# Score visits of six PSUM banks across head pairs, in a fused attention and low-rank mixer kernel

## The chip, the cores and the metric

The kernel runs on one NeuronCore of a Trainium2 chip. Five engines take part, each with its own instruction stream: TensorE (PE, with its weight loads as PEld) multiplies matrices into the eight banks of PSUM, VectorE (DVE) and ScalarE (ACT) empty those banks, GpSimd (POOL) issues the input loads, and SyncE (SP) issues the transposing DMAs and the stores. Engines wait for each other through semaphores. The metric is the device time of one execution in microseconds; smaller is better.

## The reference

Eight batches, eight heads, 576 tokens of 64 elements, and 16 beacon keys and values that stand ahead of the tokens. First attention with a causal mask on the tokens, then a low-rank mix over the token axis, then a two-layer MLP, with two residual sums:

```python
k_all = concatenate([beacon_k, k], axis=2); v_all = concatenate([beacon_v, v], axis=2)
a = softmax(where(causal, -1e9, q @ k_all.T / sqrt(64)))
x = (a @ v_all)  # heads side by side: 8 x 576 x 512
u = x + (x.T @ U @ V).T            # U: 576 x 32, V: 32 x 576
out = u + relu(u @ w_ch1) @ w_ch2  # 512 -> 2048 -> 512
```

## The kernel before

Work goes by head pairs. A pair is two heads of a batch, four pairs to a batch, 32 in all; one pass of the loop at L896 is a slot, and slot p ends with the attention output of pair p done. Batches are numbered from 0.

**Scores.** For a pair, the transposed scores (keys down the partitions, queries along the columns) fall into four groups of 496, 464, 496 and 208 columns for each of the two heads (`groups`, L82). The third group packs pieces of three key chunks. `score_units` (L317) makes a visit of two groups: four PSUM banks (two groups by two heads), then the matmuls (L345), which use 64 rows of the array for each head, then four exponentials on ScalarE (L351), each of which empties one bank into `expt`. So a pair has two visits: groups 0 and 1, then groups 2 and 3. After both, `masks` (L321 and L323) sets what lies above the diagonal on VectorE. Four `expt` buffers hold two pairs.

**V products.** `av_unit` (L370) multiplies a head's `expt` with its values into one bank `po` (15 matmuls, L374); VectorE takes the reciprocal of the sums (L382) and writes the scaled result into `xb` (L383).

**Mixing.** When a batch is complete, `mix_units` (L395) gives four steps. `turn` has SyncE transpose `xb` into `uT` by five DMAs (L402). `head`, the first mixing products, multiplies `xb` with U into bank `qtp`, in four column strips of the array (L411). `most`, the second mixing products, multiplies that with V into four banks `ups` (L436), and VectorE adds them to `uT` in place (L423), so that this addition needs the transposes. `end` does the last 80 tokens (L449).

**MLP.** The rows of all batches form nine blocks of 512. A block is 32 units: 16 `g_unit` (four matmuls of 512 columns into `gps`, L511, then a ReLU on ScalarE, L524, or VectorE, L526) and 16 quarter units `c_unit` (four matmuls into `cps`, L537; after the fourth, an addition on VectorE, L550, and a store by SyncE, L556). The first `g_unit` of a block also transposes the block's `uT` back for that addition (`ut`, four DMAs, L505).

**Order.** All five engines keep the order in which the program writes the instructions. MLP units wait in a list `queue`; `fill(n)` takes n entries out of it and writes them. A slot writes its visits, V products and masks in turn, with nine queue entries spread between. `mix` (L746) puts the first and second mixing products into that list, the first behind 10 entries, the second behind two more, and adds empty entries. `feed` appends the blocks whose rows are complete. `pst` (L105) hands out the eight PSUM banks: a new tile takes the bank that was put on the list of emptied ones longest ago.

**Loads.** For batches 4 and up, `load_whole` (L615) loads keys and queries two batches ahead, and `turns` (L627) transposes them by ten DMAs on SyncE (L635), five in the last slot of a batch and five in the first slot of the next. `load_batch` (L607) loads the values (L217) once the V products of the batch before last have been read. The SyncE stream holds, in one order, the stores, `ut`, these ten transposes and `turn`.

Of the kernel before, what the change touches and what calls it, by code (L numbers as in the profile page):

```python
# [11 lines left out]
F32 = mybir.dt.float32  # L12
I32 = mybir.dt.int32
AF = mybir.ActivationFunctionType
# [4 lines left out]
P = 128  # L19
# [11 lines left out]
def kernel(  # L31
# [13 lines left out]
    nc = tc.nc  # L45
    B, H, S, D = q.shape
# [6 lines left out]
    NH2 = H // 2  # L53
    E = D + 1
    SK = S + Nb
    scale = float(1.0 / (D ** 0.5))
# [13 lines left out]
    SLOT = 496  # L70
# [5 lines left out]
    for c in (1, 2, 3):  # L76
# [5 lines left out]
    groups = [  # L82
        [(0, 0, q0[4], 0)],
        [(1, q0[1], S - q0[1], 0)],
        [(2, q0[2], S - q0[2], 0), (0, q0[4], nq[4], S - q0[2]), (4, q0[4], nq[4], S - q0[2] + nq[4])],
        [(3, q0[3], S - q0[3], 0)],
    ]
    gw = [max(o + w for _, _, w, o in g) for g in groups]
# [16 lines left out]
    def pst(shape, dtype, name):  # L105

        b = emptied.pop(0)
        t = psum.tile(shape, dtype, tag=f"bank{b}", name=name)
        bank_of[id(t)] = (b, t)
        return t  # L110

    def emptying(t):
        emptied.append(bank_of.pop(id(t))[0])
# [43 lines left out]
    NE = 4  # L157
    expts = [const.tile([P, EW], F16, name=f"expt{i}", tag=f"expt{i}") for i in range(NE)]
    kTs = [const.tile([P, NH2, NC * P], F16, name=f"kT{i}", tag=f"kT{i}") for i in range(2)]
# [157 lines left out]
    def score_units(c, qT, kT, ex, early=False):  # L317

        def mask_head(i):
            e4 = ex[i][:, 0:EW].rearrange("p (g w) -> p g w", w=SLOT)[:, :, 0:P]  # L320
            nc.vector.tensor_tensor(out=e4, in0=e4, in1=bigmask, op=ALU.min)  # L321
            o, n = blk[(4, 4)], nq[4]
            nc.vector.tensor_tensor(  # L323
                out=ex[i][0:n, ds(o, n)], in0=ex[i][0:n, ds(o, n)], in1=mask[0:n, 0:n], op=ALU.min
            )

        def visit(gs, idle=0, by_head=True, between=None):
            turn = [(g, i) for i in range(2) for g in gs] if by_head else [(g, i) for g in gs for i in range(2)]
            ps = {(g, i): pst([P, 512], F32, name=f"sps{i}") for g, i in turn}
            keep_warm(ps[gs[0], 0], idle)  # L330
            if early:
                for g in gs:
                    for i in range(2):
                        for ch, qa, w, o in groups[g]:
                            if ch in (g, 4):
                                n = nq[ch]
                                nc.tensor.matmul(  # L337
                                    ps[g, i][:, ds(o, n)], identb, negmask[:, min(ch, 1), 0:n],
                                    start=ch == g, stop=False, skip_group_check=True,
                                )  # L340
            for g in gs:
                for ch, qa, w, o in groups[g]:
                    for i in range(2):
                        hp = slice(D * i, D * i + D)
                        nc.tensor.matmul(  # L345
                            ps[g, i][:, ds(o, w)], kT[hp, c, ds(P * ch, P)], qT[hp, c, ds(qa, w)],
                            start=not early, stop=True, skip_group_check=early,
                        )

            def exps(g, i):  # L350
                nc.scalar.activation(  # L351
                    out=ex[i][:, ds(SLOT * g, gw[g])], in_=ps[g, i][:, 0 : gw[g]], func=AF.Exp, scale=scale
                )

            for n, (g, i) in enumerate(turn):
                if between and n == len(gs):
                    between()
                exps(g, i)
                emptying(ps[g, i])

        def masks():
            for i in () if early else range(2):
                mask_head(i)

        return [
            lambda idle=0, between=None: visit([0, 1], idle, between=between),
            lambda gs=[2, 3], by_head=True: visit(gs, 0, by_head), masks,
        ]

    def av_unit(b, h, ex, vs, xb):  # L370
        po = pst([P, NT, E], F32, name="po")
        for j in range(NT):
            for c in range(j + 1):
                nc.tensor.matmul(  # L374
                    po[:, j, :],
                    ex[0 : nk[c], ds(blk[(c, j)], P)],
                    vs[0 : nk[c], ds(c * H * E + h * E, E)],
                    start=(c == 0),
                    stop=(c == j),
                )  # L380
        r = rec[:, b * H + h, :, :]
        nc.vector.reciprocal(out=r, in_=po[:, :, D : D + 1])  # L382
        nc.vector.tensor_tensor(  # L383
            out=xb[:, :, ds(h * D, D)], in0=po[:, :, 0:D], in1=r.broadcast_to([P, NT, D]), op=ALU.mult
        )
        emptying(po)
# [216 lines left out]
    NP = B * NH2  # L603
    NBLK = B * S // 512
    Ls, qTs, xbs = {}, {}, {}
# [77 lines left out]
    def qkT_of(p):  # L683
# [8 lines left out]
            turns[0] = beacons_apart(turns[0], Ls[0][0][0], 0)  # L692
        return qkT_units(turns, qTs[b], kTs[b % 2], c, copies)

    def scores_of(p):
        b, c = divmod(p, NH2)
        return score_units(c, qTs[b], kTs[b % 2], [expts[(2 * p + i) % NE] for i in range(2)], p < NM)

    def av_of(p):
        b, c = divmod(p, NH2)  # L700
        if c == 0:
            xbs[b] = xbp.tile([P, NT, DM], F16, name="xb", tag="xb")
        return [
            lambda i=i: av_unit(b, 2 * c + i, expts[(2 * p + i) % NE], vss[b % 2], xbs[b]) for i in range(2)
        ]


    NF = 2
    NM = 5
    AHEAD = 16  # L710

    DT0 = 4
    LAG = 10
    HINT = 5

    FIRST = [3, 3, 2, 1]
# [4 lines left out]
    queue = []  # L721
    state = {"t": 0}

    def fill_turns(tr, n):
        for u in tr[:n]:
            u()
        del tr[:n]

    def fill(n):
        while n > 0 and queue:  # L730
            u = queue.pop(0)
            if u is not None:
                u()
            n -= 1

    def feed(b):

        while state["t"] < NBLK and 512 * (state["t"] + 1) <= S * (b + 1):
            t = state["t"]
            units, state["part"] = mlp_units(  # L740
                512 * t, 512, lambda i, m, t=t: rows[ds(512 * t + P * i, m), :], t % 2, t > 0, t == NBLK - 1
            )
            queue.extend(units)
            state["t"] += 1

    def mix(b):  # L746

        turned = b >= NF
        turn, head, parts = mix_units(xbs[b], S * b, turned)
        if turned:  # L750
            turn()
        n = 0 if not turned else LAG + 3 if b == B - 1 else min(LAG, len(queue) - 8)
        k = 2 if turned else 1
        most, end = parts
        rest = queue[n + k + 3 :]
        queue[:] = queue[0:n] + [head] + queue[n : n + k] + [most] + queue[n + k : n + k + 3] + [end]
        for _ in range(4):
            queue.extend(rest[:1] + [None])
            del rest[:1]
        queue.extend(rest)  # L760
        feed(b)

    with tc.manual_schedule(engines={ENG.PE, ENG.Activation, ENG.DVE, ENG.SP, ENG.Pool}):
# [11 lines left out]
        t0, sc = qkT_of(0), scores_of(0)  # L775
# [9 lines left out]
        sc = scores_of(1)  # L785
# [20 lines left out]
        for p in range(2):  # L806
# [4 lines left out]
            av = av_of(p)  # L811
            av[0]()
            sc = scores_of(p + 2)
# [79 lines left out]
            fill(1)  # L893
        regroup_of(NP1 + 2)
        tr = []
        for p in range(NP1, NP):  # L896
            b, c = divmod(p, NH2)
            if c == 0 and b + 1 < B:
                load_batch(b + 1)
            if c == (2 if b + 2 == DT0 else 1) and DT0 <= b + 2 < B:  # L900
                load_whole(b + 2)
            if c == 0 and b + 1 == DT0:
                tr = turns(b + 1)
            if c == NH2 - 1 and DT0 < b + 2 < B:
                tr = turns(b + 2)
            sc = scores_of(p + 1) if p + 1 < NP else []
            qk = qkT_of(p + 2) if p + 2 < min(NP, DT0 * NH2) else []
            av = av_of(p)
            if c == NH2 - 1 or c == 0 and b + 1 == DT0:
                fill_turns(tr, NT)  # L910
            if c == 0 and b > NF:
                mix(b - 1)
            if c == (1 if b + 1 == DT0 else 0):
                fill_turns(tr, NT)
            seq = sc[0:1] + av[0:1] + qk[0:1] + sc[1:3] + qk[1:2] + av[1:2]
            if p + 3 < min(NP, DT0 * NH2):
                seq.append(lambda p=p: regroup_of(p + 3))
            quota = QUOTA.get(b, 9)
            done = 0
            for i, u in enumerate(seq):  # L920
                u()
                want = quota * (i + 1) // len(seq)
                fill(want - done)
                done = want
# [109 lines left out]
```

## Time and profile before

| what | value |
|---|---|
| median of 3 runs | 355.72 us (355.67 to 355.79) |
| the profiled execution | 355.51 us, its span 353.9 us |
| TensorE busy | 347.2 us, 3110 matmuls |
| VectorE, ScalarE, GpSimd busy | 187.8, 166.2, 97.6 us |
| score matmuls (L345) | 34.3 us, 384 matmuls |
| exponentials (L351) | 111.1 us, 256 |
| slots 16 to 31 | about 130 to 262 us from the span's start |

The span runs from the first to the last instruction; the execution's own time is 1.6 us longer. Busy times are of one execution. The chain that ended last is followed back from the last instruction: at each step to what released it, or to the instruction before it on its engine. "Landing" is the time from a DMA's issue to its completion. An idle time in square brackets stands ahead of an instruction and names what ended it.

### The profile page before, as it was taken

The numbers are of one execution on the slowest core, as the hardware profiler recorded it, in microseconds if no ns is written. First come the engines' busy times: TensorE is split into PE (matmuls) and PEld (weight loads), VectorE is DVE, ScalarE is ACT, GpSimd is POOL, SyncE is SP. The second block draws the span as 40 slices with busy tenths as digits, with TensorE's granted clock in tenths as the row PEclk, the third lists the DMA queues.
The fourth block names the chain that finished last, engine by engine and source line by source line (L and its number), as shares of the span: only waits on it lengthen the run. The fifth ranks groups of instructions, "written<-read, shape, count | busy, mean of one in ns | idle before, by whom it ended". The sixth has DMA issues, their size and how long they took to land.

```text
span 353.9 us, 7832 instructions
## 1 busy us (share of the span) xinstructions
PE 347.2 (98%) x3110; PEld 173.5 (49%) x3110; DVE 187.8 (53%) x484; ACT 166.2 (47%) x359; POOL 97.6 (28%) x137
## 2 busy tenths in 40 slices
PE   8999999999999999999999999999999999999995
PEld 3665555455554444544444444444554444444443
DVE  4756964678967643754464457444736522313311
ACT  5967851487733663457535654466403203301400
POOL 8966803527447047305810500000000000000000
PEclk9999999999999999999999999999999999999999
DMA  9999999999999979997999992172014213013012
GB/s 181 93 195 174 157 197 172 225 143 154 111 165 148 177 101 128 163 180 89 147 139 200 130 141 65 59 109 52 31 61 102 57 59 109 12 59 101 21 58 69
DMA packets 146636, 41.89 MB, mean 118 GB/s; under 512 B 131488, under 2 KB 142080, under 8 KB 146592
## 3 DMA queue, kind: packets, MB, share of 16 engines
q0 software_dynamic: 87440, 18.18, 67.2%
q1 hardware_dynamic: 58928, 22.84, 35.5%
q8 instruction: 26, 0.43, 0.5%
q10 hardware_dynamic: 224, 0.30, 0.3%
q14 instruction: 18, 0.15, 0.2%
HBM read 37.37 MB, written 9.44 MB: 132 GB/s over the span
## 4 chain that ended last, share of the span: by engine, by line
PE 94%; DMA 2%; DVE 2%; issue 1%; ACT 1%; POOL 0%; POOLq 0%; DVEq 0%
PE gps L511 36%; PE cps L537 35%; PE po L374 9%; PE sps L345 8%; DMA st<-in_k_dram 2%; PE tps L274 1%; PE tps L280 1%; PE cph L563 1%; PE qtp L411 1%; PE sps L337 1%; PE ups L436 1%; PE ups L390 0%; DVE kT L307 0%; DVE qT L307 0%; ACT expt L351 0%
## 5 line engine op out<-in xcount | busy, mean ns | idle before, releaser
L351 ACT ACTIVATE expt<-sps 128x496 f16<-128x496 f32 (+2 forms) x256 | 111.1, 542 | 59.7 <-PE sps L345 59.7
L511 PE MATMUL gps<-uT,w 128*128 128x512 f16 x576 | 135.7, 379 | 0.1
L537 PE MATMUL cps<-w,gT 128*128 128x512 f16 x560 | 132.5, 379 | 0.0
L524 ACT ACTIVATE gT<-gps 128x512 f16<-128x512 f32 x86 | 51.9, 608 | 92.4 <-PE gps L511 90.6
L511 PEld LDWEIGHTS <-w 128*128 128x128 f16 x576 | 51.8, 98 | 59.4 <-issue 3.8
L537 PEld LDWEIGHTS <-gT 128*128 128x128 f16 x560 | 49.9, 98 | 59.3 <-issue 7.0
L526 DVE TENSOR_SCALAR gT<-gps 128x512 f16<-128x512 f32 x58 | 40.0, 690 | 47.4 <-PE gps L511 46.3
L550 DVE TENSOR_TENSOR ob<-cps,ut 128x512 f32<-128x512 f32 x31 | 21.4, 690 | 47.4 <-PE cps L537 44.4
L217 POOL DMA_DIRECT2D vs<-in_v_dram x50 | 39.5, 806 | 18.3 <-PE gps L511 4.8
L374 PEld LDWEIGHTS <-expt 128*128 128x128 f16 (+1 forms) x960 | 36.1, 98 | 14.6 <-issue 2.2
L374 PE MATMUL po<-vs,expt 128*128 128x65 f16 (+1 forms) x960 | 39.4, 194 | 0.3 <-DVE expt L321 0.3
L345 PE MATMUL sps<-qT,kT 64*128 64x80 f16 (+4 forms) x384 | 34.3, 282 | 0.6 <-DVE qT L307 0.3
L383 DVE TENSOR_TENSOR xb<-po,rec 128x320 f16<-128x320 f32 x64 | 31.5, 492 | 2.2
L321 DVE TENSOR_TENSOR expt<-expt,bigmask 128x512 f16<-128x512 f16 x54 | 22.6, 419 | 11.0 <-ACT expt L351 11.0
L382 DVE RECIPROCAL rec<-po 128x5 f32<-128x5 f32 x64 | 12.0, 188 | 25.7 <-PE po L374 25.5
L345 PEld LDWEIGHTS <-kT 64*128 64x128 f16 x384 | 11.9, 94 | 22.4 <-issue 14.4
L199 POOL DMA_DIRECT2D vs<-in_beacon_v_dram x8 | 4.3, 534 | 61.2 <-PE po L374 61.2
L623 POOL DMA_DIRECT2D st<-in_q_dram x20 | 16.9, 871 | 3.5 <-DMA vs<-in_v_dram 3.3
L423 DVE TENSOR_TENSOR uT<-ups,uT 128x496 f16<-128x496 f32 x24 | 14.5, 667 | 6.0 <-PE ups L436 3.6
L623 POOL DMA_DIRECT2D st<-in_k_dram x20 | 16.9, 879 | 0.2 <-DMA vs<-in_v_dram 0.2
L307 DVE COPY qT<-tps 128x576 f16<-128x576 f16 (+1 forms) x16 | 11.8, 735 | 3.3 <-PE tps L280 1.9
L307 DVE COPY kT<-tps 128x576 f16<-128x576 f16 (+1 forms) x16 | 11.7, 734 | 2.7 <-PE tps L280 1.9
(92 smaller groups left out, 142.6 us busy)
## 6 DMA issues: line engine op xcount, KB each, us to landing
out_dram<-ob SPq DMA_DIRECT2D x35, 256.0 KB, 2.3
vs<-in_v_dram POOLq DMA_DIRECT2D x18, 128.0 KB, 7.4
w<-in_moe_w_ch_dram POOLq DMA_DIRECT2D x4, 512.0 KB, 6.3
w<-in_moe_w_ch_dram POOLq DMA_DIRECT2D x2, 1024.0 KB, 13.9
st<-in_k_dram POOLq DMA_DIRECT2D x12, 128.0 KB, 7.2
st<-in_q_dram POOLq DMA_DIRECT2D x12, 128.0 KB, 9.8
st<-in_k_dram POOLq DMA_DIRECT2D x2, 576.0 KB, 13.0
st<-in_q_dram POOLq DMA_DIRECT2D x2, 576.0 KB, 16.2
```

Source lines behind the costliest of these rows:

```text
L217: nc.gpsimd.dma_start(out=dst[a : a + nq[j], j, :, :], in_=src[hs, ds(q0[j], nq[j]), :].rearrange("h p d -> p h d"))
L307: copy(out=whole[:, :, ds(w * a, w)], in_=ps[:, 0 : TP * w].rearrange("x (j p) -> x p j", j=w),)
L321: nc.vector.tensor_tensor(out=e4, in0=e4, in1=bigmask, op=ALU.min)
L345: nc.tensor.matmul(ps[g, i][:, ds(o, w)], kT[hp, c, ds(P * ch, P)], qT[hp, c, ds(qa, w)], start=not early, stop=True, skip_group_check=early,)
L351: nc.scalar.activation(out=ex[i][:, ds(SLOT * g, gw[g])], in_=ps[g, i][:, 0 : gw[g]], func=AF.Exp, scale=scale)
L374: nc.tensor.matmul(po[:, j, :], ex[0 : nk[c], ds(blk[(c, j)], P)], vs[0 : nk[c], ds(c * H * E + h * E, E)], start=(c == 0), stop=(c == j),)
L383: nc.vector.tensor_tensor(out=xb[:, :, ds(h * D, D)], in0=po[:, :, 0:D], in1=r.broadcast_to([P, NT, D]), op=ALU.mult)
L511: nc.tensor.matmul(g[:, 0:n], w1[:, cc, ts(dc, P)], uT[:, cc, ds(t0, n)], start=(cc == 0), stop=(cc == NCC - 1))
L524: nc.scalar.activation(out=gT["t"][:, dc, 0:n], in_=g[:, 0:n], func=AF.Relu)
L526: nc.vector.tensor_scalar_max(out=gT["t"][:, dc, 0:n], in0=g[:, 0:n], scalar1=0.0)
L537: nc.tensor.matmul(ps[:m, :], gT["t"][:, dc, ds(P * i, m)], w2[:, dc, :], start=(dc == 0), stop=turned and dc == NDC - 1, skip_group_check ...
L623: nc.gpsimd.dma_start(out=dst[a : m[j], j, :, :], in_=src[:, ds(q0[j], nq[j]), :].rearrange("h p d -> p h d"))
```

## The change

From slot 16 (batch 4) on, slots are written by `long_slot`, in a cycle of three slots with four visits:

- A visit fills six banks: three groups by two heads, and the groups of a visit may belong to two pairs. Scores of pairs 17 to 31 take 20 visits; they took 30. Each exponential still empties one bank. Visits of pair p + 2 begin in slot p.
- The mixings of batches 3 to 6 no longer go through `mix`. `mix_between` issues `turn` and holds the other steps: the first mixing products follow directly behind the next visit, the second come at a fixed place of a slot once at least 8 (`SINCE`) units have been written since `turn`, the last 80 tokens three queue entries later. The mixing of batch 7 is as before.
- V products have one MLP unit between the two heads, and one between the second and the next visit; masks come at fixed places.
- Slots write 6, 6 and 13 units in turn, where each had nine entries, some of which were mixing steps or empty.

Everything up to slot 15 is as before. The diff, cut to its core:

```diff
+    def visit(parts):
+        at = {p: (p % NH2, qTs[p // NH2], kTs[p // NH2 % 2], expts_of(p)) for p, _ in parts}
+        ps = {(p, g, i): pst([P, 512], F32, name=f"sps{i}") for p, g in parts for i in range(2)}
+        for p, g in parts:
+            c, qT, kT, _ = at[p]
+            for ch, qa, w, o in groups[g]:
+                for i in range(2):
+                    hp = slice(D * i, D * i + D)
+                    nc.tensor.matmul(
+                        ps[p, g, i][:, ds(o, w)], kT[hp, c, ds(P * ch, P)], qT[hp, c, ds(qa, w)],
+                        start=True, stop=True,
+                    )
+        for p, g in parts:
+            for i in range(2):
+                nc.scalar.activation(
+                    out=at[p][3][i][:, ds(SLOT * g, gw[g])], in_=ps[p, g, i][:, 0 : gw[g]], func=AF.Exp, scale=scale
+                )
+                emptying(ps[p, g, i])
...
+    SINCE = 8
...
+        def mix_between(b):
+            turn, head, parts = mix_units(xbs[b], S * b)
+            turn()
+            mixing[:] = [head] + parts
+            state["since"] = 0
+            feed(b)
+        def go(n):
+            fill(n)
+            state["since"] += n
+        def visit_then_head(parts):
+            parts = [(p, g) for p, g in parts if p < NP]
...
+            visit(parts)
+            if len(mixing) == 3:
+                mixing.pop(0)()
+        def between_visits():
+            if len(mixing) == 2 and state["since"] >= SINCE:
+                mixing.pop(0)()
+                queue.insert(3, mixing.pop(0))
+        def long_slot(p, av):
+            r = (p - P6) % 3
+            if r == 0:
+                visit_then_head([(p + 1, 0), (p + 1, 1), (p + 1, 2)])
+            go(2)
+            if r and p < NP:
+                masks_of(p)
+            between_visits()
+            go(3 if r == 2 else 2)
+            av[0]()
+            go(1)
+            av[1]()
+            if p % NH2 == NH2 - 1 and p + 1 < NP:
+                mix_between(p // NH2)
+            go(1)
+            if r == 0:
+                visit_then_head([(p + 1, 3), (p + 2, 0), (p + 2, 1)])
+            elif r == 1:
+                visit_then_head([(p + 1, 2), (p + 1, 3), (p + 2, 0)])
+            else:
+                visit_then_head([(p + 1, 1), (p + 1, 2), (p + 1, 3)])
+                go(2)
+                between_visits()
+                go(2)
+                if p + 1 < NP:
+                    masks_of(p + 1)
+                go(2)
...
-            if c == 0 and b > NF:
-                mix(b - 1)
+            if c == 0 and b > NF and p <= P6:
+                (mix if p < P6 else mix_between)(b - 1)
...
+            if p >= P6:
+                long_slot(p, av_of(p))
+                continue
```

## The prediction

> **What bounds the kernel.** I read the page's totals first, then the chain of waits in order of time from 80 us on, then the transposes that the mixing needs (how long each takes to land), then VectorE and the sync queue around the mixings. Batches are counted from 0, so the changed stretch is batches 4 to 7, slots (head pairs) 16 to 31; "mix 4" is the mixing of batch 4.
>
> ```profile
> PE 347.2 (98%) x3110; PEld 173.5 (49%) x3110; DVE 187.8 (53%) x484; ACT 166.2 (47%) x359; POOL 97.6 (28%) x137
> ...
> PE 94%; DMA 2%; DVE 2%; issue 1%; ACT 1%; POOL 0%; POOLq 0%; DVEq 0%
> ```
>
> TensorE is the bound, and from 110 us on the chain is TensorE alone but for the last store. So a change pays only by taking time out of TensorE's own stream, and costs whatever it makes TensorE wait.
>
> ```profile
> 164.64 0.51 PE sps L345 x4
> 165.16 0.97 PE gps L511 x4
> ...
> 166.58 1.73 PE gps L511 x8
> 168.31 0.41 PE sps L345 x8
> ```
>
> The chain: each piece is a start, a length, a line. A first visit moves 496 + 464 columns for two heads side by side; four matmuls of 512 columns normally take 0.866, so 960 columns take 0.40, and the piece takes 0.51. The four matmuls after it take 0.97, not 0.866. Each visit thus pays 0.11 on the way in and 0.105 on the way out.
>
> ```profile
> 103.70 0.40 PE qtp L411 x20
> 104.10 0.51 PE sps L345 x4
> 104.61 0.97 PE cps L537 x4
> ...
> 107.87 0.68 DVE uT L423
> 108.55 0.04 issue
> 108.59 0.25 PE sps L345
> 108.83 2.70 PE cps L537 x12
> ```
>
> The same chain at mix 2 shows two things. A first mixing product next to a visit keeps both entry costs (0.40 and 0.51) and shares one exit. And a visit just behind the second mixing products (ups) stands until VectorE has added the first of them to uT (L423) and so freed its bank: the matmul starts 0.04 after that addition ends.
>
> ```profile
> L402 SPq DMA_TRANSPOSE uT<-xb x2: 1335/1341/1347, 132.7 to 134.1; - x2
> DMA to landing us min/median/max: 8.2/8.2/8.2
> L402 SPq DMA_TRANSPOSE uT<-xb x2: 1575/1662/1750, 170.6 to 172.2; - x2
> DMA to landing us min/median/max: 7.5/7.6/7.6
> L402 SPq DMA_TRANSPOSE uT<-xb x2: 1267/1302/1336, 203.6 to 205.0; - x2
> DMA to landing us min/median/max: 6.7/7.1/7.6
> ```
>
> Third and fourth transposes of mixes 3, 4 and 5. L423 needs the first four, so it can start at 134.1 + 8.2 = 142.3, at 172.2 + 7.5 = 179.7, and at 205.0 + 6.7 = 211.7.
>
> ```profile
> 179.85 2.42 DVE L423 TENSOR_TENSOR uT<-ups,uT 128x496 f16<-128x496 f32 x4 [2.35 <-DMA uT<-xb]
> 213.82 2.42 DVE L423 TENSOR_TENSOR uT<-ups,uT 128x496 f16<-128x496 f32 x4 [2.14 <-PE ups L436]
> 154.78 5.34 SPq L505 DMA_TRANSPOSE ut<-uT  x4
> 160.28 2.11 SPq L635 DMA_TRANSPOSE kT<-st  x1
> ```
>
> VectorE at mixes 4 and 5, and the sync queue ahead of mix 4. At mix 4 the landing already decides: the addition waited for it until 179.85, 0.35 longer than TensorE alone (ups at 179.15) made it. Before the change this stays hidden: the next visit takes four banks, 3.3 us behind ups. The cover is thin.
>
> **The parts and their costs.** The order of the built program has the same matmuls on TensorE, in other places.
>
> Visits: 30 become 20, the columns stay. 10 x (0.11 + 0.105) = 2.15 saved.
>
> First mixing products behind a visit (mixes 3 to 6): before, cps, qtp, cps; now sps, qtp, gps. By the rows at 103.70 one exit of 0.105 goes each time: 0.4 saved. Together **2.6 saved**, all of it on the path.
>
> V products: before as now a full unit of 0.87 lies between them and a visit. Nothing.
>
> ScalarE: six exponentials (before four). Four take 1.96 with overlap, six about 2.8; a unit's ReLU behind them waits at most that. The shortest distance between visits is six units, 5.3 us, and eight banks go round in turn, so I cost it at nothing; cover gone, at most 2.8 - 1.96 = 0.8 a visit.
>
> Second mixing products: this is the term that matters. They come 8 queue units after the turn is issued, before it was 12, and a six-bank visit follows. In the built order that visit takes all four ups banks, the bank of an output addition and of a V product, in VectorE's order behind L423. So what is late is the transposes, then L423, then the output addition, reciprocal and xb behind it on VectorE, then the visit.
>
> Mix 3. Both programs are alike up to 130.32. From there by rows: visit 1456 columns 0.71, qtp 0.40, 32 matmuls of 0.2165 = 6.93, two V products 0.92, visit 0.60, two exits 0.21: ups at 140.1 (before 144.83). The transposes were issued at 130.18, ahead of the change: landed 142.3. L423 ends at 143.0, 143.6, 144.2, 144.8; xb of the first V product at 145.5, the output addition at 146.1, the second xb at 146.7. TensorE reaches the visit at 144.2 (ups 0.32, twelve matmuls with an exit 2.7, V products 0.92, uend 0.14) and would have left it at 144.8; it leaves at 146.3, and the next cps, due at once, waits for the second xb until 146.8: 2.0, and with the release of 0.04 a bank **2.1 lost**.
>
> Mix 4. From ups to ups: 120 matmuls 25.98, eight V products 3.66, five visits 3.12, products 0.86, exits 0.65 = 34.3, plus 2.1: ups at 176.4. The turn is held by the sync queue: the last store of block 2, ut, five key/query transposes (L635), then the turn. That block's last cps ends at 155.5 (before 153.49), so all of it moves by 2.0: issue at 169.8, the fourth landed at 181.7. A V product needs the first ups bank: TensorE is there at 180.0, the bank at 182.4; the visit then ends at 186.1, not 184.4: **4.1 lost**.
>
> Mix 5. By the same sums block 3's last cps ends at 194.8; the store, ut and five L635 (6.9 us at 188.20 before) now all precede the turn: issue at 208.3, its fourth at 212.4, landed with the 6.7 of before at 219.1. Counted instead from the V loads that contend with it (197.40 to 211.7 = 14.3; they now start at 204.4) 218.7. I take 218.9. Ups at 215.7, visit reached at 219.0; L423 and an output addition free its banks until 222.0: **2.7 lost**.
>
> Mix 6. No loads are left (landed in 2.4 at 236 us); VectorE's own chain costs about 0.2.
>
> Landing times in the new places are in no row. Bounds: 2.4 (uncontended, 236 us) and 9.6 (200.9 us). At 2.4 mixes 4 and 5 lose 0.2 together, at 9.6 they lose 6.2 and 5.8. I take the rows of the same mixes, since the loads move with the turns.
>
> Sum: 2.1 + 4.1 + 2.7 + 0.2 - 2.6 = +6.5. The profiled execution took 355.51 (span 353.9), against a median of 355.72; 355.51 + 6.5 = **362.0**.
>
> **A rule weighed.** The granted clock stayed at 1.00 through mix 2's stall (107 to 109 us, 0.49 idle), while the eight opening matmuls after idleness took 631 ns, where L511 has 379. The Trainium skill, "TensorE: Matmul & The Clock Gate", section "Part 1: The HAM clock gate", says that TensorE's clock halves after an idle window of about 3.4 us. By the row the sum stays 362.0; by the rule it stays too unless the waits fill such a window, and then it is that of the clock rival below.
>
> **The rivals.**
> *In time (faster).* The transposes land early enough that L423 never holds a bank. For: 2.4 at mix 6. Against: the three rows of 6.7 to 8.2, mix 3's being of a turn that the change does not touch. At 4.0 each, mix 3 loses nothing, mix 4 about 0.6, mix 6 0.2: 355.5 - 2.6 + 0.8 = 353.7. It decides when the three stalls together are below 2.6, with landings of about 6.
> *Partly late.* Mix 3 as recorded, but mixes 4 and 5 land in 5 to 6 us, since the turns now start later after other traffic: 2.1 + 2.2 + 0.8 + 0.2 - 2.6 = +2.7, 358.2.
> *Later still.* Five more transposes stand ahead of mix 5's turn, and the key loads overlap mix 4's: at 9.6, 2.1 + 6.2 + 5.8 + 0.2 - 2.6 = +11.7, 367.2.
> *Clock.* Mix 4's 2.4 us wait and the 1.7 just after make TensorE cold for eight matmuls, at 631 - 379 = 252 ns each: +2.0, and once more at mix 5: 366.0. Against: 1.00 at 107 us.
>
> **How the numbers follow.** Forecast 0.52, partly late 0.20, later still 0.11, clock 0.06, in time 0.08, something between (partly late with mix 3 mended) 0.03. The range takes in most of partly late and the lower half of the two upper cases: 357.6 to 366.0. About 0.2% (0.7 us) is what a measurement of this kernel can tell from no change. Faster 0.08, same 0.03, slower 0.89.
>
> **What would show it.** Right: 20 visits, TensorE busy about 2.6 us less in sum, its idle time grown by 6 to 12 us in three places near 144, 180 and 219 us, where score matmuls (at mix 4 a V product first) wait for VectorE's additions (uT, ob) and xb, and the first of those additions for the DMA uT<-xb. Wrong: L423 starting within 0.4 us of ups at mixes 3 and 4; waits of sps on ScalarE instead; the granted clock below 1.00 after 180 us.

## The result and the profile after

The changed kernel takes 364.83 us (median of 4 runs, 363.82 to 366.12) against 355.74 us before (4 runs, 355.67 to 355.79) on the same chip: a ratio of 1.0258, 95% interval 1.0224 to 1.0291. It is slower by about 9 us; 362.0 was predicted, with a range of 357.6 to 366.0. The profiled execution is the slowest of the four, 366.12 us with a span of 364.5, so it is 10.6 us longer than the profiled one of before and just above that range. In the new file the visit's matmuls are L379, the V products L394, the scaled result `xb` L403, `turn` L422, the first mixing products L431, the addition to `uT` L443, the second mixing products L456, and the MLP's products L531 (`gps`) and L557 (`cps`).

The page of the changed kernel: totals, the granted clock in forty slices, and the shares of the chain that ended last.

```profile
PE 349.5 (96%) x3110; PEld 175.8 (48%) x3110; DVE 187.9 (52%) x484; ACT 165.8 (45%) x359; POOL 97.5 (27%) x137
...
PEclk9999999999999999999969999999999999999999
...
PE 82%; DMA 6%; DVE 4%; SPq 3%; ACT 2%; issue 1%; DVEq 0%
```

TensorE's share of the chain fell from 94% to 82%, and DMA, VectorE and SyncE's queue took its place. One slice has a granted clock under full speed. TensorE's busy time rose, although there are fewer visits; part of that is the slice at a lower clock, where the same matmuls are busy for longer.

What TensorE waited for between 128 and 290 us (total, times, longest); for the kernel before, the same list is empty:

```profile
PE po L394 <- DVE uT L443: 4.7, 1, 4.7
PE sps L379 <- DVE uT L443: 2.0, 6, 0.8
PE sps L379 <- DVE ob L570: 0.5, 2, 0.3
PE sps L379 <- DVE xb L403: 0.4, 1, 0.4
PE cps L557 <- DVE xb L403: 0.3, 1, 0.3
```

A V product waits once, for 4.7 us, and score matmuls wait in pieces, each time for VectorE: for the addition to `uT`, or for the output addition and the V products' scaling that stand behind it. None waits for ScalarE, which had six exponentials in a row to do. VectorE's additions (the bracket is the idle time before them and what ended it):

```profile
142.91 2.42 DVE L443 TENSOR_TENSOR uT<-ups,uT 128x496 f16<-128x496 f32 x4 [1.93 <-PE po L394]
184.48 2.42 DVE L443 TENSOR_TENSOR uT<-ups,uT 128x496 f16<-128x496 f32 x4 [7.36 <-DMA uT<-xb]
222.40 2.42 DVE L443 TENSOR_TENSOR uT<-ups,uT 128x496 f16<-128x496 f32 x4 [5.94 <-PE sps L379]
```

TensorE had written the second mixing products from 140.16, 176.79 and 218.81 on. So the additions began 2.8, 7.7 and 3.6 us behind them. At mix 4 the profile names the DMA. At mixes 3 and 5 it names an engine, and the landing has to be read beside it. The second to fourth transposes of mix 3, the second to fourth of mix 4, and the fourth of mix 5:

```profile
L422 SPq DMA_TRANSPOSE uT<-xb x3: 1279/1327/1342, 131.2 to 133.9; - x3
DMA to landing us min/median/max: 7.4/8.7/8.9
...
L422 SPq DMA_TRANSPOSE uT<-xb x3: 1303/1417/1809, 171.6 to 174.4; - x3
DMA to landing us min/median/max: 8.5/8.6/10.0
...
L422 SPq DMA_TRANSPOSE uT<-xb x1: 1310/1310/1310, 217.7 to 217.7; - x1
DMA to landing us min/median/max: 4.6/4.6/4.6
```

The fourth of mix 3 was issued at 133.91 and took 8.88: 142.8, and the addition starts at 142.91. The fourth of mix 4 was issued at 174.38 and took 9.98: 184.36. The fourth of mix 5 was issued at 217.72 and took 4.55: 222.28, and the addition starts at 222.40. So at all three mixings the addition starts about 0.1 us after the fourth landing. The chain of waits in order of time, from the visit ahead of mix 4 to the one after it:

```profile
167.19 0.60 PE sps L379 x6
167.79 0.40 PE qtp L431 x20
168.19 0.98 PE gps L531 x4
...
174.38 9.98 DMA uT<-xb
...
184.48 0.69 DVE uT L443
185.17 0.04 issue
185.21 0.98 PE po L394 x15
186.19 1.71 PE cps L557 x4
187.90 1.09 PE sps L379 x10
```

The first three lines are what the first mixing products behind a visit look like: both entries (0.40 for qtp) and one exit (0.98 where 0.87 is the bare unit), as the row at mix 2 had let expect. The last three are slow: fifteen matmuls of a V product take 0.98 (0.46 elsewhere), four cps matmuls 1.71. The windows around them (length; busy times of PE, PEld, DVE, ACT and POOL; granted clock; DMA share; GB/s):

```profile
182.00:183.00 1.00, 0.00 (x0) 0.00 (x0) 0.00 (x0) 0.00 (x0) 0.68 (x1) 0.91 2.75 72
183.00:184.00 1.00, 0.00 (x0) 0.00 (x0) 0.00 (x0) 0.00 (x0) 0.00 (x0) 0.50 1.08 77
...
189.00:190.00 1.00, 1.00 (x4) 0.37 (x5) 0.14 (x1) 1.00 (x4) 0.00 (x0) 0.68 1.92 146
```

TensorE is idle from 180.47 on. From about 182.8 its clock is 0.50, and at about 189.6 it is back (a second at 0.91 is 0.18 of it at half speed, one at 0.68 is 0.64). So there are two candidates for the time at mix 4, the late transposes and the clock, and the experiments have to part them.

### The profile page after: what moved, and what is told of

Its sections match the earlier page's. It is cut to its first block, busy times and chain, and to the rows that moved or that the text cites. A ratio compares the mean times of both kernels' runs of the same rounds, so it can differ in the third digit from the quotient of the medians.

```text
span 364.5 us, 7841 instructions
## 1 busy us (share of the span) xinstructions
PE 349.5 (96%) x3110; PEld 175.8 (48%) x3110; DVE 187.9 (52%) x484; ACT 165.8 (45%) x359; POOL 97.5 (27%) x137
## 4 chain that ended last, share of the span: by engine, by line
PE 82%; DMA 6%; DVE 4%; SPq 3%; ACT 2%; issue 1%; DVEq 0%
PE gps L531 31%; PE cps L557 31%; PE po L394 7%; DMA uT<-xb 5%; PE sps L345 4%; PE sps L379 3%; SPq L422 2%; DVE uT L443 2%; ACT expt L351 1%; PE tps L274 1%; SPq L655 1%; PE cph L583 1%; DMA stq<-in_q_dram 1%; PE tps L280 1%; PE qtp L431 1%
## 5 line engine op out<-in xcount | busy, mean ns | idle before, releaser
L531 PE MATMUL gps<-uT,w 128*128 128x512 f16 x576 | 135.2, 379 | 0.1
L557 PE MATMUL cps<-w,gT 128*128 128x512 f16 x560 | 131.9, 382 | 0.3 <-DVE xb L403 0.3
L557 PEld LDWEIGHTS <-gT 128*128 128x128 f16 x560 | 51.1, 98 | 60.9 <-issue 6.3
L531 PEld LDWEIGHTS <-w 128*128 128x128 f16 x576 | 52.0, 98 | 57.9 <-issue 2.1
L394 PEld LDWEIGHTS <-expt 128*128 128x128 f16 (+1 forms) x960 | 36.5, 98 | 19.2 <-issue 7.0
L394 PE MATMUL po<-vs,expt 128*128 128x65 f16 (+1 forms) x960 | 39.8, 194 | 5.0 <-DVE uT L443 4.7
L403 DVE TENSOR_TENSOR xb<-po,rec 128x320 f16<-128x320 f32 x64 | 31.4, 491 | 2.2
L443 DVE TENSOR_TENSOR uT<-ups,uT 128x496 f16<-128x496 f32 x24 | 14.5, 665 | 17.1 <-DMA uT<-xb 7.4
L379 PE MATMUL sps<-qT,kT 64*128 64x80 f16 (+2 forms) x180 | 17.2, 288 | 2.9 <-DVE uT L443 2.0
L345 PE MATMUL sps<-qT,kT 64*128 64x496 f16 (+3 forms) x204 | 18.4, 282 | 0.7 <-DVE qT L307 0.3
L379 PEld LDWEIGHTS <-kT 64*128 64x128 f16 x180 | 6.8, 96 | 15.0 <-issue 11.2
```

The costliest lines, as they stand in the source:

```text
L345: nc.tensor.matmul(ps[g, i][:, ds(o, w)], kT[hp, c, ds(P * ch, P)], qT[hp, c, ds(qa, w)], start=not early, stop=True, skip_group_check=early,)
L379: nc.tensor.matmul(ps[p, g, i][:, ds(o, w)], kT[hp, c, ds(P * ch, P)], qT[hp, c, ds(qa, w)], start=True, stop=True,)
L394: nc.tensor.matmul(po[:, j, :], ex[0 : nk[c], ds(blk[(c, j)], P)], vs[0 : nk[c], ds(c * H * E + h * E, E)], start=(c == 0), stop=(c == j),)
L403: nc.vector.tensor_tensor(out=xb[:, :, ds(h * D, D)], in0=po[:, :, 0:D], in1=r.broadcast_to([P, NT, D]), op=ALU.mult)
L531: nc.tensor.matmul(g[:, 0:n], w1[:, cc, ts(dc, P)], uT[:, cc, ds(t0, n)], start=(cc == 0), stop=(cc == NCC - 1))
L557: nc.tensor.matmul(ps[:m, :], gT["t"][:, dc, ds(P * i, m)], w2[:, dc, :], start=(dc == 0), stop=turned and dc == NDC - 1, skip_group_check ...
```

## The experiments

The theory on trial: the second mixing products come too early for the transposes, VectorE's addition waits and holds the ups banks, and the visit behind it waits for those. Rivals: the six-bank visit itself, or the order of the slots, is what costs; or the clock is.

**1. The second mixing products later: e1_since14.** One constant.

```diff
-    SINCE = 8
+    SINCE = 14
```

> The changed kernel with SINCE = 14 in place of 8: the second mixing products come 14 to 16 units after their turn. Late transposes (theory): each turn has landed by then, the waits of TensorE at the three mixings go, and the saving of switches is left: 355.5 - 2.6 + 0.4 for VectorE's own chain, 353.0 to 353.6. Six-bank visits as such (rival: six exponentials, or six banks asked of eight, stop TensorE wherever the mixing lies): the time stays above 360. Both by half: 357 to 359.

Measured: 353.95 us (353.82 to 354.09, 4 runs), 0.9951 of before (0.9934 to 0.9967). TensorE's list of waits is empty between 128 and 300 us, and the additions start right behind the second mixing products (146.76, 181.85 and 215.29):

```profile
147.17 2.42 DVE L443 TENSOR_TENSOR uT<-ups,uT 128x496 f16<-128x496 f32 x4
182.27 2.42 DVE L443 TENSOR_TENSOR uT<-ups,uT 128x496 f16<-128x496 f32 x4 [2.06 <-PE ups L456]
216.00 2.41 DVE L443 TENSOR_TENSOR uT<-ups,uT 128x496 f16<-128x496 f32 x4
```

The landings are as late as before: the fourth transpose of mix 4 takes 9.3 us and lands at 180.50, but now ahead of the second mixing products. All six-bank visits are still there. So the visits, the masks and the V products of the change cost little by themselves (0.9 us at two visits, as shown under the savings below): it is the place of the second mixing products that turns a gain of 1.9 us into a loss of 9. This kernel is faster than the one before and than the changed one.

**2. The place kept, the dependence removed: e2_turn_apart.** The transposes of mixes 3 to 6 go into rows of `uT` that are no longer used, and the addition reads rows of batch 1 in their place, so the residual of those four batches is wrong. The early place stays.

```diff
-                    out=uT[:, :, ds(u0 + q0[j], nq[j])], in_=xb[: nq[j], j, :]
+                    out=uT[:, :, ds((0 if apart else u0) + q0[j], nq[j])], in_=xb[: nq[j], j, :]
...
-                nc.vector.tensor_tensor(out=dst, in0=ups, in1=dst, op=ALU.add)
+                nc.vector.tensor_tensor(out=dst, in0=ups, in1=old if apart else dst, op=ALU.add)
```

> The changed kernel, all DMAs as they are, but the transposes of mixes 3 to 6 write into the dead rows of batch 0 in uT, and the addition behind the second mixing products reads rows of batch 1 instead of what was transposed: the residual of four batches is left out, and no instruction waits for those landings. Late transposes: 353 to 354, the additions start within 0.1 us of ups in every mixing, granted clock 1.00 throughout. Six-bank visits as such, or VectorE's chain of additions behind ups: 360 or more.

Measured: 353.94 us (353.41 to 354.2), 0.9948 (0.9931 to 0.9965). The transposes still land late (7.7 to 9.2 us at mix 4), but nobody waits for them. One wait of TensorE is left in the stretch:

```profile
PE cps L557 <- DVE xb L403: 0.3, 1, 0.3
```

So with the same order of instructions on TensorE, waiting for the transposes is the whole loss. Against this run the changed kernel can be measured mixing by mixing, by the distance from one batch's second mixing products to the next one's (34.60, 35.10, 33.42 and 44.46 us here): 2.0 more from mix 3, 6.9 from mix 4, 3.1 from mix 5, nothing from mix 6. Together 12.0 of the 12.3 us between the two profiled executions.

**3. The turn ahead of the key and query transposes: e3_turn_first.** From batch 4 on, the five L655 transposes that SyncE held ahead of `turn` go behind it.

```diff
-            if c == NH2 - 1 or c == 0 and b + 1 == DT0:
+            if c == NH2 - 1 and p < P6 or c == 0 and b + 1 == DT0:
                 fill_turns(tr, NT)
...
-                fill_turns(tr, NT)
+                fill_turns(tr, NT if p <= P6 else 2 * NT)
```

> The changed kernel with the five key and query transposes of a batch's last slot moved behind that batch's turn, from batch 4 on: all ten stand behind it in SyncE's order. If SyncE's queue makes the turns of mixes 4 and 5 late: they are issued 3 to 4 us earlier, right after xb, the wait at mix 4 falls from some 8 us to 2 to 5 and that of mix 5 from 3 to 0 to 1, mix 3 stays: 357 to 361. If the landing is set by the loads on the same DMA engines and not by the place in the queue: the transposes land at the same moments as before the move, 363 to 366.

Measured: 357.63 us (357.12 to 358.88, 5 runs), 1.0059 (1.0031 to 1.0086). The turns of mixes 4 and 5 start at 166.48 and 201.40, where they started at 170.25 and 212.27.

```profile
178.11 2.42 DVE L443 TENSOR_TENSOR uT<-ups,uT 128x496 f16<-128x496 f32 x4 [1.76 <-PE cps L557]
213.58 2.42 DVE L443 TENSOR_TENSOR uT<-ups,uT 128x496 f16<-128x496 f32 x4 [4.00 <-DMA uT<-xb]
```

Counted against run e2 the losses are now 1.5, 0.8 and 1.1. SyncE's order, with what it sets off, was worth 7.2 us between the medians; what is left is the landing time, of 5.1 to 7.7 us at mix 4 (7.5 for the fourth transpose).

**4. The loads taken away: e4_no_v_loads.** The condition leaves out the value loads of batches 5, 6 and 7, so those of mix 3 too, against the text below, and the V products of these batches use values of others. GpSimd's queue then reaches the last key and query loads earlier (146 to 155 us), so at mix 4 no load of any kind is under way.

```diff
-            v_loads(v[b], beacon_v[b], vss[b % 2])
+            if b <= DT0:
+                v_loads(v[b], beacon_v[b], vss[b % 2])
```

> The changed kernel without the value loads of batches 6 and 7 (those batches are computed with the values of batches 4 and 5); the loads at mix 3 stay. If these loads make the transposes land late: landings of mixes 4 and 5 fall from 10 and 8 us to 3 to 6, their waits shrink by 3 to 6 us together, 356 to 361, with mix 3's 2 us left as it is. If the landing is late by the key and query loads alone or by SyncE's order: mix 5 becomes early (no other load is near), mix 4 stays, 361 to 363.

Measured: 353.94 us (353.6 to 355.08), 0.9946 (0.9929 to 0.9962). The five transposes of mix 4:

```profile
L422 SPq DMA_TRANSPOSE uT<-xb x5: 1212/1257/1265, 167.5 to 172.7; - x5
...
DMA to landing us min/median/max: 2.4/2.5/2.5
```

2.4 to 2.5 us, where the changed kernel had up to 10.0. So the landing time is the loads' doing; the run can't say how much of it is the values and how much the keys and queries. At mix 5 the turn still starts late for SyncE's order (203.51), and the addition waits 3.98 us for it.

**5 and 6. The early place at one mixing alone: e5_only_mix4 and e6_only_mix5.** For the second, `b == 5`.

```diff
+            state["enough"] = SINCE if b == 4 else 14
...
-            if len(mixing) == 2 and state["since"] >= SINCE:
+            if len(mixing) == 2 and state["since"] >= state["enough"]:
```

> The changed kernel with the second mixing products of mix 4 alone at 8 units behind the turn; those of mixes 3, 5 and 6 at 14, as with SINCE = 14 (353.95). If mix 4's 6.9 us are its own, from a landing near 10 us and a clock that falls during the wait: 358 to 361, the wait of the V product 2 to 5 us, and a granted clock below 1.00 for some microseconds behind it if the wait passes about 3 us, 1.00 if it doesn't. If most of them were inherited from mix 3's delay: 354 to 356.

> The same with mix 5 alone at its early place (10 units), mixes 3, 4 and 6 at 14 or more. If each early mixing costs by itself: 353.95 + 2.4 to 3.1, 356.3 to 357.1, the clock at 1.00. If mix 5 was late only because mixes 3 and 4 had pushed everything: 354.0 to 354.6.

Measured: mix 4 alone 360.41 us (359.64 to 361.38, 4 runs), 1.0121 (1.0104 to 1.0138), 6.5 over run e1; mix 5 alone 355.90 (354.6 to 357.11, 10 runs), 1.0000 (0.9985 to 1.0014), 1.95 over e1, less than expected. Mix 3 was not run alone; 10.9 - 6.5 - 1.95 leaves 2.4 for it, if the three add up. TensorE at mix 4 in e5, and the addition at mix 5 in e6:

```profile
181.47 0.62 PE L394 MATMUL po<-vs,expt 128*128 128x65 f16 x15 [3.46 <-DVE uT L443]
```

```profile
212.20 2.42 DVE L443 TENSOR_TENSOR uT<-ups,uT 128x496 f16<-128x496 f32 x4 [5.22 <-DMA uT<-xb]
```

In e5 the wait is 1.3 us shorter than in the changed kernel, and yet the place costs almost the same 6.5. The clock falls here as well (0.50 between 182.8 and 189.7 us), and it costs more: the 24 cps matmuls behind the visit take 7.52 us, in the changed kernel 5.63.

**7. Early second mixing products in the kernel before: e7_before_early.** Visits of four banks, the old slots, one constant of the kernel before, which moves the mixings from batch 2 on.

```diff
-    LAG = 10
+    LAG = 6
```

> The kernel before, four-bank visits and all, with LAG = 6 in place of 10: the first and second mixing products of the mixings from batch 2 on come four queue entries sooner. If the early place is what costs, whatever the visit takes: visits wait for VectorE behind the transposes here too, at mixes 4 and 5 above all, 359 to 365. If it takes a visit of six banks to make the lateness felt: 355.8 to 357.

Measured: 365.22 us (364.33 to 366.54, 4 runs), 1.0275 (1.0247 to 1.0304). Here L345, L423 and L537 are the visit, the addition and cps. What TensorE waited for from 128 to 290 us, and its clock at mix 4:

```profile
PE sps L345 <- DVE uT L423: 3.3, 6, 1.8
```

```profile
181.00:182.00 1.00, 0.49 (x7) 0.27 (x6) 1.00 (x3) 0.26 (x1) 0.00 (x0) 0.91 1.65 172
182.00:183.00 1.00, 0.75 (x3) 0.36 (x3) 1.00 (x3) 1.00 (x4) 0.00 (x0) 0.50 3.04 116
```

A visit of four banks waits for the same addition, and the kernel loses as much as the changed one. So six banks aren't needed for the loss; being early is enough. Its 9.5 us are only partly broken down. By the distance from one batch's second mixing products to the next one's, in the profiled executions, 1.7 us come from mix 3, 4.8 from mix 4 and 1.3 each from mixes 5 and 6; TensorE's waits for that addition in this stretch, the line above among them, come to 4.5 us.

**8. The first mixing products away from the visit: e8_head_apart.** On top of run e1, they come one unit behind the visit.

```diff
         def go(n):
-            fill(n)
+            fill(1)
+            if len(mixing) == 3 and state["since"] >= 1:
+                mixing.pop(0)()
+            fill(n - 1)
             state["since"] += n
```

> The changed kernel with SINCE = 14 and the first mixing products of mixes 3 to 6 one unit behind a visit, not directly behind it. By the switch rows (0.105 an exit): four exits more, 0.4 us, 354.3 to 354.4 beside the 353.95 of SINCE = 14. If a switch from score tiles to column strips costs less than one from full tiles: 0.8 us, 354.8. If nothing: 353.95.

Measured: 354.37 us (354.11 to 354.66, 5 runs), 0.9961 (0.9947 to 0.9975): 0.42 over e1, as the rows gave (four exits of 0.105). The two ran on different chips, and the intervals of their ratios overlap, so this agrees with the term rather than proves it.

**9 to 11. The clock kept up by useless matmuls: e9_warm_mix4, e10_only4_warm, e11_warm_all.** Matmuls of 192 columns, into columns of the last 80 tokens' bank that nobody reads, stand where TensorE would wait: 44 at mix 4 of the changed kernel, 38 at mix 4 of run e5, and 12, 44 and 22 at mixes 3, 4 and 5 of the changed kernel. Nothing that causes a wait is moved.

```diff
+            for _ in range(busy):
+                nc.tensor.matmul(
+                    whole[:, NCC * n : 512], w2[:, 0, 0:P], w2[:, 0, 0 : 512 - NCC * n], start=False, stop=True,
+                    skip_group_check=True,
+                )
```

> The changed kernel with 44 useless matmuls of 192 columns behind the last 80 tokens' products of mix 4, into columns of their bank that nobody reads: about 44 x 0.08 = 3.5 us of the 4.7 us in which TensorE waits there for the addition to uT. Nothing that waits is moved. If the half clock after that wait costs by the rows (about 2.2 us): the granted clock stays at 1.00, the first units behind the wait take what they take elsewhere (four cps 0.87, a visit 0.61), and the time falls by about 2.2 to 362.6. If the wait alone is what costs, the time stays at 364.8; if the dummy work is in the way, it rises by up to 3.5.

> The kernel with the early place at mix 4 alone (360.4), with 38 such useless matmuls (3.0 of the 3.46 us of waiting). If the half clock is what lies between the 3.5 us of waiting and the 6.5 us that this place costs: the granted clock stays at 1.00 and the time falls by about 3 to 357.4. If only the waits count: 360.4. If the dummy work delays: up to 363.4.

> As the run with 44 useless matmuls at mix 4, whose six times fell into two groups, 361.3 to 362.8 at a mean clock of 1.00 and 364.7 to 365.9 at 0.994 to 0.995; here 12 more such matmuls (1.0 us) stand behind the last 80 tokens' products of mix 3 and 22 (1.8 us) behind those of mix 5, inside the waits of the visit that follows there. If the clock of the second group fell at mix 3 or mix 5: no such group, every clock at 0.997 or more and a median of about 362.2, so 2.6 under the changed kernel, and the clock is shown to be worth that. If it fell elsewhere, or if the group has another cause (a later landing at mix 4): two groups again, median about 363.7. If the useless work is itself in the way: above 364.

Measured: e9 363.73 us (361.34 to 365.9, 6 runs), 1.0229 (1.0190 to 1.0268); e10 359.66 (359.28 to 359.81, 4 runs), 1.0111 (1.0096 to 1.0126); e11 363.22 (362.27 to 364.7, 5 runs), 1.0209 (1.0196 to 1.0223). The clock was 1.00 throughout the changed stretch in the profiled executions of e9 and e10. In e9's six it was 1.00 three times (361.3 to 362.8) and 0.994 to 0.995 three times (364.7 to 365.9); in e11's five it was 0.997 to 1.00, and no time is above 364.7. So the lower clock of e9's second group did not show in these five when the waits of mixes 3 and 5 were filled too. Not all of the spread is the clock: the execution of 364.7 us had 0.998, and it was already 1.3 us behind the profiled changed kernel at the second mixing products of mix 2 (108.57 against 107.23), ahead of the changed stretch.

The chains of the profiled e5 and e10 differ mainly in one place, the 24 cps matmuls behind the visit at mix 4. The first fence is e5's chain, the second e10's:

```profile
185.17 7.52 PE cps L557 x24
```

```profile
185.26 5.29 PE cps L563 x24
```

That is 2.2 us, and the two executions are 2.1 apart. Between the medians it is only 0.75, with ratios of 1.0121 and 1.0111, and e11 is 1.6 under the changed kernel, with intervals that all but touch (1.0223 and 1.0224). So the clock is worth somewhere between 0.5 and 2 us, not the expected 2.2 to 3, and the medians alone don't settle even that; filling the waits leaves 363.2, still 9.3 us over run e1. The waits for the transposes are the bulk.

## Why the prediction was right, and where it was off

**Direction and mechanism: right.** The waits stand where it put them (score matmuls at mixes 3 and 5, a V product first at mix 4), behind VectorE's addition, which waits for the transposes; e2 takes that dependence away, and 12 of 12.3 us go. TensorE's idle time grew by 8.3 us, within the 6 to 12 forecast. Its busy time did not fall by 2.6 us: it rose by 2.3 in the changed kernel, partly by the half clock. The signs named as wrong (waits on ScalarE, an addition within 0.4 us of ups at mixes 3 and 4) did not appear; the third, the clock under 1.00 after 180 us, did.

**Savings, 2.6 predicted: the term was right in size, but not "all of it on the path".** Runs e1 and e2 show 1.9 and 1.9 between the medians, and the profiled e1 is 1.7 under the profiled kernel before. The 0.4 of the first mixing products agrees with e8. What is missing stands in run e1's chain, at the visit behind the last 80 tokens of mix 5:

```profile
219.55 0.50 DVE xb L403
220.05 0.05 issue
220.10 0.37 PE sps L379
```

The two heads' matmuls of a group otherwise start together. Here the last one waits until VectorE has scaled a V product and so freed its bank, and the visit takes 1.03 us (219.43 to 220.46) where such a visit needs 0.60. At mix 6 the same happens, 1.05 us where 0.62 are needed. That is 0.86 of the 0.9 that the profiled e1 lacks. So the ten visits are worth about what was forecast; TensorE's busy time fell by 1.8 in e1 (347.2 to 345.4).

**Mix 3: 2.1 predicted, 2.0 measured.** The rows carried over, because the turn is the same in both programs: landed at 142.8 against 142.3, the addition at 142.91.

**Mix 4: 4.1 predicted, 6.9 measured. This is the term that was mis-sized,** and the step is "issue at 169.8, the fourth landed at 181.7". The issue was close (170.25). The landing was 184.36, because the fourth transpose took 10.0 us, not the 7.5 of the same mix before. The reason given for the row, "the loads move with the turns", holds only in part: before, the fourth was issued 9.1 us behind the start of the value loads (163.09 to 172.2), after the change 7.9 (166.50 to 174.4). Counted from the start of the loads, as the step for mix 5 did, it would have landed 16.6 behind it as before, at 183.1, and that was nearer. So the V product waited 4.74 us, not 2.4. The rest of that term, 1.7 for the visit behind it, is about right: with the clock at 1.00 (e10) the visit stands 2.13 us where 0.61 is needed, 1.5 lost.

**Mix 5: 2.7 predicted, 3.1 measured, and this is near partly by luck.** The second mixing products came 3.1 us later than forecast (218.8, not 215.7), mostly for the 2.8 of mix 4. The turn started at 212.27, not 208.3, and its first DMA held SyncE's queue for 2.8 us, so the fourth was issued at 217.72, not 212.4: 5.3 later. But it landed in 4.55 us, where the row of before had 6.7, and the two errors nearly cancel: the distance from ups to the addition, 3.2 predicted, is 3.6. What held is the step's other count, from the start of the value loads: they started at 207.66, and 14.3 behind that is 222.0, where 222.28 was measured.

**Mix 6: 0.2 predicted, 0 measured**, with landings of 2.4 to 3.1 us.

**The rivals.** "Later still" had the landing of mix 4 right (9.6 there, 10.0 measured) and that of mix 5 wrong (4.6). "Partly late" had mix 5's landing nearly right (5 to 6) but not its cost (0.8), because the transposes were issued so much later. "Clock" was given 0.06 as an alternative; it came on top. Its 252 ns a matmul were of the right order (211 by the four cps matmuls that took 1.71), its place was not: in the changed kernel's profile the half clock ran mainly while the visit had to wait for VectorE's releases anyway. From the V product's start to the end of the 24 cps behind the visit that kernel took 9.41 us (185.21 to 194.62), e9 and e10 at full clock 8.9 (184.48 to 193.39, 181.65 to 190.55): 0.5 on the path, although the slow rows alone, summed against their normal lengths, are 2.2 longer. In e5 the clock came back later against the work, and the same thing cost 2.3. "In time" is what run e1 makes of the change: 353.95, where that rival had 353.7.

So the profiled execution took 10.6 us more, not 6.5: 2.8 from mix 4, 0.4 from mix 5, 0.9 of gain that was not there in the profiled e2 (353.79 against 355.51) and 0.3 that I could not place, less 0.3 at mixes 3 and 6. The median is 1.3 below it, and so 2.8 above the forecast.

The rule of the Trainium skill that was weighed, "TensorE: Matmul & The Clock Gate", "Part 1: The HAM clock gate", says that half clock follows an idle window of about 3.4 us. The wait of 4.74 us is longer than that, but the clock fell 2.3 us into it (180.47 to 182.8). Run e7 goes further: there TensorE's longest wait was 1.84 us, with matmuls before and after it, and the clock still fell to 0.50 at about 181.8. So by the measurement a wait need not fill such a window.

## What to carry to other kernels

When an instruction is moved earlier, look at what its reader on the next engine waits for, not only at its own operands: an addition in place, which also reads a DMA's result, holds its PSUM banks from the moment the product is written until the DMA lands. Size that landing from the start of the transfers it shares the DMA engines with, and not from the row of the old place, and count the DMAs that stand ahead of it on its queue. And let a change that mixes a saving with a move be tried with the move alone taken back: here one constant gave 0.9951 in place of 1.0258.

## What the runs showed of the hardware

- A transpose of `xb` landed in 2.4 to 2.5 us with no load under way (e4 at mix 4; the changed kernel at mix 6, but for a first one of 3.1) and in 4.6 to 10.0 beside the loads that GpSimd issues (the changed kernel at mixes 3 and 4). The Trainium skill, "Trainium Kernel Development and Optimization", section "Key Constraints", says that DMAs of the SyncE, ScalarE and GpSimd queues run on the same 16 DMA engines and interleave. These runs agree: the transposes are on SyncE's queue, the loads on GpSimd's.
- The granted clock was at 0.50 for about 6.8 us in the changed kernel (182.8 to 189.6) and in e5 (182.8 to 189.7), and for about 3.4 in e7 (181.8 to 185.2), and it changed in one step. In each case the 3.41 us ahead of the fall (as long as the half clock of e7) had TensorE busy for only 1.06, 1.37 and 1.43 us (changed kernel, e5, e7), while a stretch with 2.01 us busy (e5, 176.01 to 179.43) brought no fall. In e5 it fell only after TensorE was back at work (181.47), and so hit work more than waiting: 2.3 us there against 0.5 in the changed kernel. It may be part of the wide spread of e9; that was not shown.
- Waiting time filled with useless matmuls kept the clock at 0.997 or more in all five executions of e11. As a cure that gives at most about 1.6 us here; moving the work (e1) gives 10.9.
